# Eight pairs prepared on TensorE, staged early, with the next pair's PV blocks put off by one iteration

## The chip, the cores and the metric

The kernel runs on one core of a Trainium2 chip. The metric is the device time of the whole program in microseconds (us). The profile's span, from the first to the last instruction, is 1.8 us shorter than the time of the same execution. A program on one core has no die to compare with; a run is called slow when it is over 1.5% above the fastest run of the same kernel. Comparisons of times here use fast runs. A ratio is the mean time of one kernel's fast runs over the mean of the other's fast runs of the same rounds on the same chip, so it is not quite the ratio of the medians that are quoted.

## The reference

Attention over 8 batches and 8 heads, with q pooled in pairs of rows, then a feed-forward network (FFN) without an activation:

```python
q_pool = q.reshape(B, H, S // 2, 2, D).mean(axis=3)       # 8 x 8 x 576 x 64
scores = (1 / sqrt(D)) * q_pool @ k.T                     # 576 x 1152 per head
attn = softmax(scores)
x = (attn @ v), heads put side by side                    # 4608 x 512
a, b = x @ w1, x @ w2                                     # 4608 x 1024
out = ((a * b) @ w3) @ w_out                              # 4608 x 512
```

## The kernel before

Heads go in 32 pairs, four pairs to a batch. Each pair has k (kT) and pooled q (qT) transposed, then scores, exponentials (ScalarE), PV (the product with v) and a normalization. The main loop has 162 iterations. Each issues two chunks of scores and of exponentials, the PV blocks whose exponentials are ready, and as a filler some matmuls of the FFN, counted out by a pace in us. One `po` tile holds PV's sums, two `psc` tiles the scores, two `ff` banks everything else.

```python
def prep_dma(P):                      # pairs 6 to 31: transposed by DMA
    new_kq(P)
    kc = ab.tile([128, NJ, 2, D], FP16, tag="kc", bufs=2, name="kc")
    nc.vector.tensor_copy(out=kc..., in_=kst.pop(P))
    nc.sync.dma_start_transpose(out=kT[P], in_=kc...)
    pool_q(P)                         # VectorE adds neighbouring rows
    nc.sync.dma_start_transpose(out=qT[P], in_=qps[pp][o:o + 64]...)
    copy_v(P)

def prep_pe(P):                       # pairs 0 to 5: transposed on TensorE
    new_kq(P); pool_q(P)
    kc = ...; nc.vector.tensor_copy(out=kc..., in_=kst.pop(P))
    ...                               # 9 transposes of q, 9 of k into two ff banks
    nc.vector.tensor_copy(out=qT[P]..., in_=t2[:, 128:704])
    ...                               # kT blocks 0 to 7, block 8
    copy_v(P)

for it in range(NIT):
    ...                               # scores, expo, twice
    due = (due if filler else busy - T_SC) + (PACE0 if it < 20 else PACE1)
    lead = 0.5 if prepped < NPE else 2.0
    if prepped < NP and it * 2 * CH >= (prepped - lead) * PAIR + 2 * CH:
        if prepped < NPE:
            fill(0, settle=True)
        prep(prepped)
        ...                           # loads of a later pair
    for J, i in ready:
        attend(J, i)                  # PV
        if J % NJ == NJ - 1 and i == 4:
            normalize(J // NJ)
            fill(due)
    fill(due)
```

(Cuts are marked with `...`.) `qp` is the pooled q, `kc` the k put in order, `xn` the normalized sums of PV, `xT` the same transposed, which the FFN reads; `gT` is a * b, and T the product of w3 and w_out. `NPE` is the number of pairs that go through TensorE. After the loop come the last PV, what is left of the FFN and two FFN units that need the last batch (the tail).

The softmax here doesn't subtract the row's maximum and nothing guards it: scores larger than these inputs give would overflow.

## Time and profile before

| | before |
|---|---|
| time, 4 runs | 464.77 us median (460.99 to 467.72) |
| span of the profiled run | 462.8 us, mean granted TensorE clock 0.987 |
| TensorE busy | 422.5 us |
| ScalarE busy | 329.8 us |
| TensorE waits for the DMA that makes qT | 8.7 us, once |

How to read it: TensorE's busy time is 91% of the span. ScalarE has 29% to spare, so what counts is where TensorE waits. The prediction below shows the lines. A further line of the profile before, which the prediction did not use, is needed later. It is from the view of busy time by stretches: the stretch in us, its length, then busy time and count of instructions by engine, then the granted TensorE clock, the DMA share and GB/s.

```profile
61.70:65.10 3.40, 2.96 (x29) 2.27 (x29) 2.17 (x5) 0.46 (x1) 0.80 (x2) 0.50 1.18 208
...
95.80:102.60 6.80, 2.87 (x27) 1.65 (x27) 0.00 (x0) 1.94 (x2) 0.00 (x0) 0.50 1.26 144
```

Apart from its start and end, the program ran TensorE at half its clock (0.50) twice, both in the ramp: during the preparation near 62 us, and at the end of and after the wait for qT.

### The profile page before, as it was taken

The numbers are of one execution on the slowest core, as the hardware profiler recorded it, in microseconds if no ns is written. First come the engines' busy times: TensorE is split into PE (matmuls) and PEld (weight loads), VectorE is DVE, ScalarE is ACT, GpSimd is POOL, SyncE is SP. The second block draws the span as 40 slices with busy tenths as digits, with TensorE's granted clock in tenths as the row PEclk, the third lists the DMA queues.
The fourth block names the chain that finished last, engine by engine and source line by source line (L and its number), as shares of the span: only waits on it lengthen the run. The fifth ranks groups of instructions, "written<-read, shape, count | busy, mean of one in ns | idle before, by whom it ended". The sixth has DMA issues, their size and how long they took to land.

```text
span 462.8 us, 11974 instructions
## 1 busy us (share of the span) xinstructions
PE 422.5 (91%) x5132; PEld 222.4 (48%) x5132; DVE 195.6 (42%) x340; ACT 329.8 (71%) x350; POOL 69.6 (15%) x107
## 2 busy tenths in 40 slices
PE   2868888839999999999999999999999999999995
PEld 1544445425555555555555555555555555544442
DVE  2243355405544544355435543554355434444130
ACT  3868646728888888888888888888888888813332
POOL 7322112201111111111111111111100000000000
PEclk9999989979999999999999999999999999999999
DMA  8999996998999989999979999989973251022303
GB/s 135 209 192 208 208 205 84 147 137 115 122 123 201 154 138 117 165 182 137 145 141 171 133 127 177 172 111 142 183 138 52 53 120 38 15 58 47 77 15 91
DMA packets 98052, 59.99 MB, mean 130 GB/s; under 512 B 69840, under 2 KB 87248, under 8 KB 98000
## 3 DMA queue, kind: packets, MB, share of 16 engines
q0 software_dynamic: 25168, 33.56, 47.4%
q1 hardware_dynamic: 72832, 25.68, 35.8%
q8 instruction: 40, 0.66, 0.6%
q14 instruction: 12, 0.10, 0.1%
HBM read 67.11 MB, written 9.44 MB: 165 GB/s over the span
## 4 chain that ended last, share of the span: by engine, by line
PE 80%; DVE 9%; DMA 5%; ACT 3%; issue 2%; POOL 0%; ACTq 0%; POOLq 0%
PE po L204 22%; PE psc L185 20%; PE pp L299 12%; PE pa L276 12%; PE pb L289 11%; DVE xn L216 5%; DMA qT<-qp 4%; ACT er L191 2%; PE pT L263 2%; DVE rz L214 1%; DMA kst<-in_k_dram 1%; PE w3t L248 1%; DVE kT L162 1%; DVE qT L158 1%; DVE qp L119 0%
## 5 line engine op out<-in xcount | busy, mean ns | idle before, releaser
L191 ACT ACTIVATE er<-psc 128x1024 f16<-128x1024 f32 x324 | 313.4, 1021 | 83.6 <-PE psc L185 79.6
L204 PEld LDWEIGHTS <-er 128*128 128x128 f16 x2880 | 99.2, 98 | 55.3 <-issue 35.9
L185 PE MATMUL psc<-qT,kT 64*128 64x512 f16 (+7 forms) x1152 | 109.5, 291 | 15.0 <-DMA qT<-qp 8.7
L185 PEld LDWEIGHTS <-kT 64*128 64x128 f16 x1152 | 43.3, 95 | 88.3 <-issue 72.6
L289 PE MATMUL pb<-xT,w2sb 128*128 128x512 f16 x288 | 79.7, 379 | 0.7 <-DVE gT L294 0.7
L276 PE MATMUL pa<-xT,w1sb 128*128 128x512 f16 x288 | 80.0, 381 | 0.0
L294 DVE TENSOR_TENSOR gT<-pb,asb 128x512 f16<-128x512 f32 x72 | 49.6, 689 | 69.0 <-PE pb L289 68.6
L299 PE MATMUL pp<-T_73,gT 128*128 128x512 f16 x288 | 70.1, 379 | 0.0
L285 DVE COPY asb<-pa 128x512 f32<-128x512 f32 x56 | 38.6, 689 | 55.3 <-PE pa L276 55.2
L90 POOL DMA_DIRECT2D kst<-in_k_dram x32 | 22.9, 715 | 231.1 <-DVE kc L135 195.5
L308 DVE TENSOR_SCALAR osb<-pp 128x512 f32<-128x512 f32 x28 | 19.3, 691 | 57.0 <-PE pp L299 53.7
L289 PEld LDWEIGHTS <-w2sb 128*128 128x128 f16 x288 | 25.7, 97 | 24.1 <-issue 1.7
L299 PEld LDWEIGHTS <-gT 128*128 128x128 f16 x288 | 25.5, 97 | 24.5
L276 PEld LDWEIGHTS <-w1sb 128*128 128x128 f16 x288 | 25.8, 98 | 23.1 <-issue 0.3
L204 PE MATMUL po<-vt_78,er 128*128 128x65 f16 x720 | 30.6, 195 | 2.3 <-DVE xn L216 1.8
L204 PE MATMUL po<-vt_77,er 128*128 128x65 f16 x720 | 31.3, 197 | 1.0 <-DVE xn L216 0.6
L204 PE MATMUL po<-vt_79,er 128*128 128x65 f16 x720 | 30.1, 193 | 1.6 <-DVE xn L216 1.1
L204 PE MATMUL po<-vt_80,er 128*128 128x65 f16 x720 | 29.8, 194 | 1.2 <-DVE xn L216 0.9
L283 ACT COPY asb<-pa 128x512 f32<-128x512 f32 x16 | 9.4, 587 | 27.5 <-PE pa L276 27.5
L216 DVE TENSOR_TENSOR xn<-po,rz 128x640 f16<-128x640 f32 x32 | 26.4, 824 | 1.1
L97 POOL DMA_DIRECT2D vst<-in_v_dram x32 | 23.2, 724 | 15.6 <-DVE rz L214 5.3
L214 DVE RECIPROCAL rz<-po 128x10 f32<-128x10 f32 x32 | 7.1, 221 | 33.5 <-PE po L204 33.5
(68 smaller groups left out, 142.2 us busy)
## 6 DMA issues: line engine op xcount, KB each, us to landing
qst<-in_q_dram POOLq DMA_DIRECT2D x32, 288.0 KB, 6.3
kst<-in_k_dram POOLq DMA_DIRECT2D x32, 288.0 KB, 4.9
vst<-in_v_dram POOLq DMA_DIRECT2D x32, 288.0 KB, 8.8
out_dram<-osb SPq DMA_DIRECT2D x72, 128.0 KB, 3.5
w3h<-in_moe_w_dram POOLq DMA_DIRECT2D x2, 1024.0 KB, 19.9
wosb<-in_moe_w_out_dram POOLq DMA_DIRECT2D x1, 1024.0 KB, 19.6
xT<-xn SPq DMA_TRANSPOSE x64, 4.2
w1sb<-in_moe_w_dram POOLq DMA_DIRECT2D x1, 1024.0 KB, 20.8
```

The source lines that it names most:

```text
L90: nc.gpsimd.dma_start(out=kst[P].rearrange("p u j d -> p u (j d)"), in_=k[b, h0:h0 + 2].rearrange("u (p j) d -> p u (j d)", j=NJ))
L97: nc.gpsimd.dma_start(out=vst[P].rearrange("p u j d -> p u (j d)"), in_=v[b, h0:h0 + 2].rearrange("u (p j) d -> p u (j d)", j=NJ))
L185: nc.tensor.matmul(t[:, u, o:o + ln], kT[P][s, j, :], qv[s, f0:f0 + ln], start=True, stop=True)
L191: nc.scalar.activation(out=er[:, :, r:r + CH], in_=psc.pop(c), func=AF.Exp, bias=0.0, scale=SCALE)
L204: nc.tensor.matmul(po[P][:, u, VW * i:VW * i + D + 1], er[:, u, r:r + 128], vts[P % 4][:, u, j, 0:D + 1], start=(j == 0 and i == 0), stop= ...
L216: nc.vector.tensor_tensor(out=xn.rearrange("p i u d -> p u i d"), in0=acc[:, :, :, 0:D], in1=rz.to_broadcast([128, 2, 5, D]), op=ALU.mult)
L276: nc.tensor.matmul(pa, w1sb[:, mc, ft * 128:ft * 128 + 128], xT[:, mc, t0:t0 + 512], start=(mc == 0), stop=(mc == NC - 1))
L285: nc.vector.tensor_copy(out=asb, in_=pa)
L289: nc.tensor.matmul(pb, w2sb[:, mc, ft * 128:ft * 128 + 128], xT[:, mc, t0:t0 + 512], start=(mc == 0), stop=(mc == NC - 1))
L294: nc.vector.tensor_mul(out=gT[:, ft, :], in0=pb, in1=asb)
L299: nc.tensor.matmul(pp, gT[:, ft, 128 * i:128 * i + 128], T16[:, ft, :], start=(ft == 0), stop=(ft == NF - 1))
L308: nc.vector.tensor_scalar_mul(out=osb, in0=pp, scalar1=1.0 / (SCL * SCL))
```

## The change

The intent is to take three waits away. Two batches (eight pairs) are prepared on TensorE, so the first DMA transposes come later, after the early rush of loads. VectorE's part of a preparation is issued about an iteration before TensorE's. When a pair ends, the next pair's first PV blocks wait for the next iteration, so TensorE has the FFN and the next scores to do while VectorE normalizes. The filler gets a higher pace early on, and `T_AT`, the iterations at which the two halves of T enter it, starts one earlier.

```diff
-    NPE = 6
-    T_AT = (9, 14)
+    NPE = 8
+    T_AT = (8, 14)
-    PACE0, PACE1 = 1.95, 2.19
+    PACE0, PACE1 = 2.2, 2.19
+    def prep_stage(P):
+        pool_q(P)
+        kcs[P] = ab.tile([128, NJ, 2, D], FP16, tag="kc", bufs=2, name="kc")
+        nc.vector.tensor_copy(out=kcs[P]..., in_=kst.pop(P))
+        copy_v(P)
     def prep_pe(P):
-        ...                                  # pool_q, kc and copy_v were here
-        for j in range(NJ):
+        for j in (8, 0, 1, 2, 3, 4, 5, 6, 7):   # t2 is complete first
     ...
+        at = it * 2 * CH / PAIR
+        if staged < NPE and at >= staged - 0.8:
+            prep_stage(staged)
+            ...                              # loads
+        lead = 0.5 if prepped < NPE else min(1.6, 0.5 + 0.5 * (prepped - NPE + 1))
+        if prepped < NP and at >= prepped - lead:
+            ...                              # prep_pe, or prep_dma and one load
+        last = [n for n, (J, i) in enumerate(ready) if J % NJ == NJ - 1 and i == 4]
+        if last:
+            ready = ready[:last[0] + 1]
         for J, i in ready:
             attend(J, i)
-            if J % NJ == NJ - 1 and i == 4:
-                normalize(J // NJ)
-                fill(due)
+        if last:
+            normalize(ready[-1][0] // NJ)
```

More of the change, by code (lines that the diff above doesn't have):

```diff
@@ L140, in prep_dma @@
         copy_v(P)
+    kcs = {}
+    def prep_stage(P):
+        pool_q(P)
+        kcs[P] = ab.tile([128, NJ, 2, D], FP16, tag="kc", bufs=2, name="kc")
+        nc.vector.tensor_copy(out=kcs[P].rearrange("p j u d -> p u j d"), in_=kst.pop(P))
+        copy_v(P)
     def prep_pe(P):
@@ L145, in prep_pe @@
         new_kq(P)
-        pool_q(P)
-        kc = ab.tile([128, NJ, 2, D], FP16, tag="kc", bufs=2, name="kc")
-        nc.vector.tensor_copy(out=kc.rearrange("p j u d -> p u j d"), in_=kst.pop(P))
+        kc = kcs.pop(P)
+        t2 = psum.tile([128, 1024], FP16, tag="ff", bufs=2, name="t2")
         t1 = psum.tile([128, 1024], FP16, tag="ff", bufs=2, name="t1")
-        t2 = psum.tile([128, 1024], FP16, tag="ff", bufs=2, name="t2")
         for c in range(NJ):
@@ L163, in prep_pe @@
         nc.vector.tensor_copy(out=kT[P][:, 8], in_=t2[:, 0:128])
-        copy_v(P)
-    def prep(P):
-        (prep_pe if P < NPE else prep_dma)(P)
     psc = {}
@@ L334 @@
                lambda: load(5), lambda: load(6)]
-    loaded, prepped = 7, 1
-    prep(0)
+    loaded, staged, prepped = 7, 1, 1
+    prep_stage(0)
+    prep_pe(0)
     n_units = NT // 512
@@ L371 @@
         due = (due if filler else busy - T_SC) + (PACE0 if it < 20 else PACE1)
-        lead = 0.5 if prepped < NPE else 2.0
-        if prepped < NP and it * 2 * CH >= (prepped - lead) * PAIR + 2 * CH:
-            if prepped < NPE:
-                fill(0, settle=True)
-            prep(prepped)
-            prepped += 1
+        at = it * 2 * CH / PAIR
+        if staged < NPE and at >= staged - 0.8:
+            prep_stage(staged)
+            staged += 1
             if waiting:
@@ L381 @@
                     waiting.pop(0)()
-            elif loaded < NP:
+            else:
                 load(loaded)
                 loaded += 1
+        lead = 0.5 if prepped < NPE else min(1.6, 0.5 + 0.5 * (prepped - NPE + 1))
+        if prepped < NP and at >= prepped - lead:
+            if prepped < NPE:
+                fill(0, settle=True)
+                prep_pe(prepped)
+            else:
+                prep_dma(prepped)
+                load(loaded)
+                loaded += 1
+            prepped += 1
         ready = [b for b in blocks[nb:nb + 40]
                  if b[0] * SQ + min(128 * b[1] + 128, SQ) <= 2 * it * CH]
+        last = [n for n, (J, i) in enumerate(ready) if J % NJ == NJ - 1 and i == 4]
+        if last:
+            ready = ready[:last[0] + 1]
         busy += T_AV * len(ready)
```

## The prediction

> **What bounds the kernel now.** I read first the page's busy shares and its slices, then the chain that ended last, then TensorE's waits, and last the timeline around the waits. Of the page's parts 1, 2 and 4:
>
> ```profile
> PE 422.5 (91%) x5132; PEld 222.4 (48%) x5132; DVE 195.6 (42%) x340; ACT 329.8 (71%) x350; POOL 69.6 (15%) x107
> ...
> PE   2868888839999999999999999999999999999995
> ACT  3868646728888888888888888888888888813332
> ...
> PE 80%; DVE 9%; DMA 5%; ACT 3%; issue 2%; POOL 0%; ACTq 0%; POOLq 0%
> ```
>
> TensorE (PE) carries the chain and is full from the tenth slice (104 us) on. ScalarE's exponentials need 324 x about 1.0 us, and run at eight tenths up to slice 35. So the end is TensorE's work plus whatever time TensorE loses. The losses are in three places.
>
> (a) The first transposes made by DMA. TensorE's waits have one large line, and the chain in order of time shows what it hangs on:
>
> ```profile
> PE psc L185 <- DMA qT<-qp: 8.7, 1, 8.7
> ...
> 81.56 18.13 DMA qT<-qp
> 99.73 0.71 PE psc L185 x6
> ```
>
> Pair 6 (of 32 pairs of heads; the first six are transposed on TensorE) is the first to go by DMA. Its qT was issued at 81.56 and landed at 99.69, while loads of three pairs (kst, qst, vst, issued 76.7 to 86.2) were in flight. Everything stood still from 91.0 to 99.7.
>
> (b) The preparations on TensorE in the ramp. The timeline of the last of them (line, engine, output<-input, count, in brackets the idle time before and who ended it):
>
> ```profile
> 74.47 0.69 DVE L267 CAST T_73<-pT 128x512 f16<-128x512 f32 x1 [3.08 <-PE pT L263]
> 75.19 0.76 DVE L119 TENSOR_TENSOR qp<-qst 64x1152 f16<-64x1152 f16 x1
> ...
> 76.00 0.43 PE L152 MATMUL t_1142<-ident,qp 64*128 64x64 f16 x9 [1.57 <-DVE qp L119]
> ...
> 78.32 0.62 PE L248 MATMUL w3t<-ident,w3h 128*128 128x128 f16 x8 [0.61 <-DVE kT L162]
> ...
> 79.80 1.94 ACT L191 ACTIVATE er<-psc 128x1024 f16<-128x1024 f32 x2 [3.87 <-PE psc L185]
> ```
>
> VectorE starts pooling q only when the preparation is due, behind the eviction at 74.47, and TensorE waits 1.57 us for it and 0.61 for the copies afterwards; ScalarE misses 3.87.
>
> (c) The end of each pair. PV of the next pair follows in the same iteration and waits for the normalization, which frees the only po tile:
>
> ```profile
> 233.11 0.24 PE L204 MATMUL po<-vt_77,er 128*128 128x65 f16 x2
> ...
> 233.19 1.02 PE L299 MATMUL pp<-T_73,gT 128*128 128x512 f16 x4
> 233.39 0.22 DVE L214 RECIPROCAL rz<-po 128x10 f32<-128x10 f32 x1 [2.51 <-PE po L204]
> 233.64 0.82 DVE L216 TENSOR_TENSOR xn<-po,rz 128x640 f16<-128x640 f32 x1
> ...
> 234.52 0.66 PE L204 MATMUL po<-vt_78,er 128*128 128x65 f16 x16 [0.31 <-DVE xn L216]
> ```
>
> From the last PV to the next pair's first are 1.4 us, and only four FFN matmuls (0.86 us at their pace) fill them. The printed 0.31 is too small, as ends are modelled; measured by starts 0.47 is lost.
>
> **What the Trainium skill says.** "Perfetto Trace Analysis", Identifying the Most-Contended Engine: TensorE's busy share is no measure of its distance from the peak. The trace agrees: PE shows 91%, yet a matmul of 512 columns (mean 380 ns) starts 216 ns after the one before. So I count starts. "TensorE: Matmul & The Clock Gate", Back-to-back issue gap, gives N/2.4 + 2.5 ns as the isolated gap (216 at N=512), and 131 as sustained: here it is 216 (in the tail 32 take 6.91 us), so the latter isn't seen. The same page, PE-mode transpose, says that the result lands in PSUM and costs a VectorE copy; here one transpose's record is 190 to 220 ns but they start 29 (q) and 56 (k) ns apart, and the copies are 0.46 + 0.68 + 0.21 us. "DMA: Bandwidth & Descriptors", Issuing engines are not separate DMA queues: all queues share 16 engines and interleave. The trace agrees: transposes of k land in 3.3 us at the end, where no load runs, and in 13.1 beside three.
>
> **The change part by part.** The times of iterations are my count of the trace: iteration n starts with the first of its score matmuls. Iteration 0 starts at 9.33, 8 at 26.98, 31 at 103.16, 161 at 403.77; the last PV at 406.15, the end 462.8.
>
> Startup. VectorE now copies v of pair 0 before qT. That load lands at 8.77, so qT ends near 8.8 + 0.45 + 0.46 = 9.7 and kT's last block at 9.9, where ScalarE's kT copy (to 9.27) was last. Cost 0.6: start 9.9.
>
> Iterations 0 to 7 have no filler, so ScalarE sets the pace, 2.0 to 2.05. The before's took 17.65 with 1.2 lost at the first normalization and some 0.3 at the preparation; without them 16.5. Iteration 8 starts at 26.4.
>
> Iterations 8 to 30. From steady iterations of before: one with 5 FFN matmuls and 18 PV takes 2.27, each FFN matmul more or less 0.216, each PV 0.029. One with four takes 2.06, but then the next second score waits 0.2 for ScalarE. Replaying the two kernels' loops for what each iteration issues gives the counts: the changed kernel has five preparations here (iterations 8, 13, 18, 23, 28; before four), 64 w3 transposes and 94 FFN and T matmuls by the end of iteration 30 (before 78: iteration 8 starts T earlier, and pace 2.2 for 1.95 adds). Summed with 0.77 a preparation (9 x 29 + 9 x 56 ns) and 56 ns a w3 transpose: 56.7 us, against 54.3 for before. Waits come on top. Before: 76.2 - 54.3 = 21.9, of which about 10 in iteration 30 are (a), 10 the four preparations (1.7, 2.1, 3.4, 2.8) and 1.5 normalizations. After: q and k lie pooled and copied an iteration early, and qT's copy starts after 10 of the 18 transposes; what stays is the wait for the eviction of one ff bank before the t1 transposes (about 0.6) and for the copies after (about 0.55): 5 x 1.15, plus 1 for w3 transposes: 6.8. So 56.7 + 6.8 = 63.5, and iteration 31 starts at 89.9 rather than 103.16: 13 us gained, while 16 more FFN matmuls are done.
>
> Iterations 31 to 160. Before: 300.6 for 130, of which the 26 with a normalization average 2.54 and the others 2.255. After, the iteration that ends a pair stops PV there and has 5 to 7 FFN matmuls, and the scores of the next, before the next PV: 5 x 0.216 + 0.54 = 1.6 against the 1.4 of the normalization, so no wait. All go at 2.255: 26 x 0.285 = 7.4 gained. Added: the last preparation on TensorE, 0.77 + 1.15 = 1.9. And pair 8, first by DMA, starts in iteration 36 while its scores are the second of iteration 40, 4 x 2.27 + 0.27 = 9.4 us later. In before, beside one pair of loads, kT is issued 1 us after and lands 9.7 after its issue (107.83 to 117.53), qT 0.6 later: 11.3. I charge 2. Some banks wait behind the normalization: 1. Sum: 300.6 - 7.4 + 1.9 + 2 + 1 = 298.1. Iteration 161 starts at 388.
>
> Tail. 16 FFN matmuls fewer: 59.0 - 3.5 = 55.5 from there. 25 matmuls (5.4 us) remain between the last PV and the first that needs the last pair, whose xT landed 4.9 after the last PV: no wait.
>
> End 388.0 + 55.5 = 443.5, that is 19 us less in the profile. As the small waits are guesses from what others took, and a count of this kind misses some, I take 16.5: 466.24 - 16.5 = 449.7.
>
> **The rivals.** (1) Pair 8 takes over the wait of pair 6: its lead of 4.5 iterations is the shortest of all (later pairs have 7.6). If loads 12 and 13 slow the transposes as in (a), 13 to 18 us, the wait is 4 to 9 us, and the time 453 to 457. Against it: the loads are one pair per preparation now, not three within 10 us. (2) ScalarE or the loads bound the ramp: the loads of pairs 5 and 6 land only at 59.4 and 64.0 (the queue is full up to 70), and a staging that waits for one blocks VectorE. I have their stagings at 65 and 77, so they just fit; also the first FFN matmul, at 75, against xT of pair 3 at about 73. If both fail: 453. (3) What (c) frees comes back as waits for ScalarE, as with four-matmul iterations: then the 7.4 shrink to 3, time 454. Against: ScalarE needs 2.0 in 2.255. (4) PE really sets all and TensorE's added 36 transposes (1.5 us) are a loss: only if the waits in (a) and (b) stayed, which the order of instructions speaks against.
>
> **Range and chances.** One rival alone leaves 453 to 457, so the upper end is 457; if no new wait comes, 445. 2% faster is 456.9. Before's own runs spread from 460.99 to 467.72, which blurs this. Faster by over 2%: 0.88; within: 0.11; slower: 0.01.
>
> **What would show it.** Right: no wait of TensorE for qT over 3 us, and the one there is near iteration 40 (about 110 us); transposes of q never behind qp; no wait of po for xn; iteration 31 near 90 us; full PE from about slice 3 on; ACT's exponentials ending near 391 instead of 407. Wrong: a DMA wait of over 4 us, VectorE waiting for kst or vst landings, a mean iteration over 2.28 from 31 on.

## The result, and the profile after

The changed kernel takes 450.95 us (median of 4 runs, 449.94 to 451.36), against 464.77. The ratio is 0.9704, with a 95% interval of 0.9625 to 0.9783: faster. Every run was fast. The page of its profile (span 448.8 us), parts 1, 2 and 4; PEclk is the granted clock in tenths:

```profile
PE 419.4 (93%) x5168; PEld 223.1 (50%) x5168; DVE 198.2 (44%) x347; ACT 329.8 (73%) x350; POOL 70.0 (16%) x107
...
PE   2889898998699999999999999999999999989995
ACT  2977776777388888888888888888888888823332
PEclk9999999999699999999999999999999999999999
...
PE 83%; DMA 5%; ACT 4%; DVE 4%; issue 3%; SPq 1%; POOL 0%; ACTq 0%; DVEq 0%; POOLq 0%
```

VectorE's share of the chain fell from 9% to 4%. DMA still has 5%. The weak slices of the ramp have filled, but the eleventh (112 to 123 us) has a new dent, in PE, in ACT and in the clock. What that is, TensorE's waits and the chain in order of time tell (start, length, what):

```profile
PE psc L187 <- DMA qT<-qp: 5.3, 1, 5.3
```

```profile
103.02 12.49 DMA qT<-qp
...
115.65 0.61 PE psc L187 x2
```

It is the same wait as before, now for pair 8, at iteration 40. Its cost is more than the 5.3 us. The view by stretches shows TensorE idle, and then at half clock for two windows of 3.4 us:

```profile
110.50:114.50 4.00, 0.00 (x0) 0.00 (x0) 0.08 (x1) 1.02 (x1) 0.00 (x0) 1.00 1.57 106
114.50:121.40 6.90, 5.75 (x45) 2.78 (x46) 0.62 (x2) 2.71 (x3) 0.00 (x0) 0.51 1.27 136
```

Iterations 40 and 41 take 9.00 and 3.32 us, where two usual ones take 4.5. So 7.8 us go there. The Trainium skill ("TensorE: Matmul & The Clock Gate", What's actually happening) says that an idle window of about 3.4 us halves TensorE's clock and that a busy one restores it. The trace agrees for this wait: TensorE is idle from 111.1 to 114.5, then at half clock for 6.8 us, of which the last 3.4 are busy. It also shows that the window need not be idle throughout: the stretch of 3.4 us at half clock near 62 us in before follows 3.40 us in which TensorE was busy for 1.64.

The preparation that answers to the one in the prediction (timeline, pair 3) looks like this:

```profile
38.36 0.76 DVE L119 TENSOR_TENSOR qp<-qst 64x1152 f16<-64x1152 f16 x1
...
39.14 0.46 DVE L148 COPY kc<-kst 128x1152 f16<-128x1152 f16 x1
...
41.59 0.43 PE L158 MATMUL t_684<-ident,qp 64*128 64x64 f16 x9
41.69 0.69 DVE L269 CAST T_73<-pT 128x512 f16<-128x512 f32 x1 [1.72 <-PE pT L265]
...
42.44 0.61 PE L163 MATMUL t_685<-ident,kc 128*128 128x128 f16 x8 [0.25 <-DVE T_73 L269]
```

q and k lie ready 2 us before their transposes. The transposes of q wait for nothing; those of k wait 0.25 us for the eviction of a bank, where before TensorE lost 1.57 for qp. The end of a pair:

```profile
211.03 0.72 PE L206 MATMUL po<-vt_80,er 128*128 128x65 f16 x18
211.58 1.03 PE L301 MATMUL pp<-T_73,gT 128*128 128x512 f16 x4
211.78 0.22 DVE L216 RECIPROCAL rz<-po 128x10 f32<-128x10 f32 x1 [0.93 <-PE po L206]
212.04 0.82 DVE L218 TENSOR_TENSOR xn<-po,rz 128x640 f16<-128x640 f32 x1
212.54 0.82 PE L187 MATMUL psc<-qT,kT 64*128 64x128 f16 x8
...
213.29 0.66 PE L206 MATMUL po<-vt_77,er 128*128 128x65 f16 x16
```

The scores of the next iteration now stand between the last PV and the next pair's first, and no wait for xn is printed. In the whole trace one is left (0.2 us), where there were 11 (4.5 us).

Where the 14.0 us of the span went, by the starts of iterations (the first score matmul of each):

| stretch | before | after | difference |
|---|---|---|---|
| up to iteration 0 | 9.33 | 9.90 | +0.6 |
| iterations 0 to 7 | 17.65 | 16.10 | -1.6 |
| iterations 8 to 30 (after: 16 more filler matmuls) | 76.18 | 62.20 | -14.0 |
| iterations 31 to 160 | 300.61 | 304.86 | +4.3 |
| from iteration 161 (after: 16 fewer) | 59.03 | 55.74 | -3.3 |

### The profile page after: what moved, and what is told of

Same layout as the page of the kernel before. It is cut to its first block, busy times and chain, and to the rows that moved or that the text cites. A ratio compares the mean times of both kernels' runs of the same rounds, so it can differ in the third digit from the quotient of the medians.

```text
span 448.8 us, 12036 instructions
## 1 busy us (share of the span) xinstructions
PE 419.4 (93%) x5168; PEld 223.1 (50%) x5168; DVE 198.2 (44%) x347; ACT 329.8 (73%) x350; POOL 70.0 (16%) x107
## 4 chain that ended last, share of the span: by engine, by line
PE 83%; DMA 5%; ACT 4%; DVE 4%; issue 3%; SPq 1%; POOL 0%; ACTq 0%; DVEq 0%; POOLq 0%
PE po L206 20%; PE psc L187 20%; PE pb L291 13%; PE pa L278 13%; PE pp L301 12%; ACT er L193 4%; PE pT L265 3%; DMA qT<-qp 3%; DMA vst<-in_v_dram 1%; DVE xn L218 1%; DVE kT L168 1%; PE w3t L250 1%; DMA out_dram<-osb 1%; DVE T_73 L269 0%; DVE osb L310 0%
## 5 line engine op out<-in xcount | busy, mean ns | idle before, releaser
L206 PEld LDWEIGHTS <-er 128*128 128x128 f16 x2880 | 97.5, 98 | 35.5 <-issue 32.0
L187 PEld LDWEIGHTS <-kT 64*128 64x128 f16 x1152 | 44.4, 95 | 96.0 <-issue 84.5
L278 PE MATMUL pa<-xT,w1sb 128*128 128x512 f16 x288 | 79.1, 379 | 1.2 <-DVE asb L287 0.7
L301 PE MATMUL pp<-T_73,gT 128*128 128x512 f16 x288 | 71.4, 384 | 0.0
L206 PE MATMUL po<-vt_80,er 128*128 128x65 f16 x720 | 29.6, 196 | 0.3 <-DVE xn L218 0.2
L206 PE MATMUL po<-vt_77,er 128*128 128x65 f16 x720 | 29.7, 195 | 0.0
L206 PE MATMUL po<-vt_78,er 128*128 128x65 f16 x720 | 28.7, 193 | 0.0
L206 PE MATMUL po<-vt_79,er 128*128 128x65 f16 x720 | 28.7, 193 | 0.0
L218 DVE TENSOR_TENSOR xn<-po,rz 128x640 f16<-128x640 f32 x32 | 26.4, 824 | 1.3 <-DVE rz L216 0.2
```

The source lines that it names most:

```text
L187: nc.tensor.matmul(t[:, u, o:o + ln], kT[P][s, j, :], qv[s, f0:f0 + ln], start=True, stop=True)
L206: nc.tensor.matmul(po[P][:, u, VW * i:VW * i + D + 1], er[:, u, r:r + 128], vts[P % 4][:, u, j, 0:D + 1], start=(j == 0 and i == 0), stop= ...
L218: nc.vector.tensor_tensor(out=xn.rearrange("p i u d -> p u i d"), in0=acc[:, :, :, 0:D], in1=rz.to_broadcast([128, 2, 5, D]), op=ALU.mult)
L278: nc.tensor.matmul(pa, w1sb[:, mc, ft * 128:ft * 128 + 128], xT[:, mc, t0:t0 + 512], start=(mc == 0), stop=(mc == NC - 1))
L301: nc.tensor.matmul(pp, gT[:, ft, 128 * i:128 * i + 128], T16[:, ft, :], start=(ft == 0), stop=(ft == NF - 1))
```

## The experiments

The theory: early staging shortens the ramp, the deferral of PV shortens every pair's end, more pairs on TensorE merely move the DMA wait to a later pair, and the loads are what makes it long. The rivals stand in the expectations. Times of each kernel are medians; before, in the same three jobs (e1 to e4, e5 to e10, e11 and e12), had 464.41, 465.49 and 465.53. The changed kernel was not run again in them, so a run is compared with it by the ratio to before or by the traces. The intervals of e2, e4 and e6 overlap that of the changed kernel (0.9625 to 0.9783); there the traces decide, and not the times.

**e1: the deferral alone, on the kernel before.**

```diff
+        last = [n for n, (J, i) in enumerate(ready) if J % NJ == NJ - 1 and i == 4]
+        if last:
+            ready = ready[:last[0] + 1]
         ...
         for J, i in ready:
             attend(J, i)
-            if J % NJ == NJ - 1 and i == 4:
-                normalize(J // NJ)
-                fill(due)
+        if last:
+            normalize(ready[-1][0] // NJ)
```

> Before with one part of the change alone: PV of the next pair moved to the next iteration. My account: the 26 pair ends in iterations 31 to 160 lose 0.28 us each, so that stretch falls from 300.6 to about 293.5, and the whole by 7 to 9 us (five or six pair ends of the ramp included); the DMA wait of about 9 us for pair 6 stays. Rival (waits for ScalarE take it back): a gain of 3 us or less, the stretch at 297 or more.

457.49 us (455.25 to 460.26), ratio 0.9878 (0.9814 to 0.9943): 5.7 us faster, clear of noise, though less than the 2% that the verdict "faster" asks for; 7 to 9 us were expected. The DMA wait stayed (9.3 us). Iterations 47 to 160, which hold no DMA wait in before, after, e1 or e2, took 258.7 us, against 263.2 before. So 22 pair ends gained 4.5 us. The deferral works, at some 70% of the size that the prediction would give for that stretch (22 x 0.285 = 6.3), and ScalarE did not take it back.

**e2: the change without the deferral.** The edit is e1's, the other way round.

> The changed kernel without that part: PV goes on in the same iteration after the normalization. My account: iterations 41 to 160 take 7 us longer, the whole 457 to 459 against 451. Rival: within 3 us of the changed kernel. TensorE's waits for xn come back in the profile in either case.

459.82 us (453.15 to 462.5), ratio 0.9847 (0.9733 to 0.9961), from two runs alone: the other two were slow. The verdict is unclear. The total is blurred besides: in its profile (of a fast run) the wait for qT is 1.4 us at most, but iteration 45 waits 4.8 us for xT instead. Iterations 47 to 160 are clear of both: 263.5 us, against 259.4 in the changed kernel, so 4.2 us for 22 pair ends. Of this stretch, the mean iterations in us:

| kernel | with a normalization (22) | the next (22) | the others (70) |
|---|---|---|---|
| before | 2.52 | 2.23 | 2.27 |
| e2 | 2.57 | 2.22 | 2.26 |
| after | 2.35 | 2.24 | 2.26 |
| e1 | 2.26 | 2.29 | 2.27 |

**e3: a longer lead for the first pairs by DMA.**

```diff
-        lead = 0.5 if prepped < NPE else min(1.6, 0.5 + 0.5 * (prepped - NPE + 1))
+        lead = 0.5 if prepped < NPE else 1.6
```

> The changed kernel with the lead 1.6 for pairs 8 and 9 too: pair 8's DMA transposes start in iteration 34 instead of 36. If what is left of the DMA wait is a matter of lead: TensorE's wait for qT (5.3 us in the profile) is gone, and with it the stretch at half clock after it, 6 to 8 us in all: 443 to 445. Rival (the transposes move into other loads and land later by as much): the wait stays at 3 us or more, 447 to 451.

450.53 us (450.06 to 451.09): as the changed kernel. The chain in order of time shows why:

```profile
99.89 16.78 DMA qT<-qp
```

qT of pair 8 was issued 3 us earlier and landed no earlier. The rival holds: lead won in this way is of no use. Lead by itself was not tested, because load 12 is issued with the preparation and moved forward too (its k at 98.76 instead of 101.90).

**e4: load 12 held until pair 8's qT has landed.**

```diff
                 prep_dma(prepped)
+                if loaded == 12:
+                    nc.gpsimd.tensor_copy(out=scr, in_=qT[8][:, 0, 0:1])
                 load(loaded)
```

> The changed kernel with the loads of pairs 12 and up held back until pair 8's qT has landed (GpSimd reads one column of it first). If the loads slow the transposes: kT and qT of pair 8 land about 3 to 5 us after their issue (3.3 and 2.9 are the shortest, with no load), no wait at iteration 40, 443 to 445, unless the late loads make pair 12 or 13 wait. Rival (the transposes are slow among themselves, six of them within 9 us): qT still lands 10 us or more after issue and the wait stays.

447.36 us (445.66 to 448.55), ratio 0.9654 (0.9602 to 0.9706). kT of pair 8 landed 3.4 us after its issue and qT 4.5 (before this edit 5.1 and 12.5), and the wait at iteration 40 is gone. So the loads slow the transposes. But the held loads came in a burst, and pair 7's xT landed 11.4 us after issue: a wait of 2.6 us at iteration 45. Iterations 45 and 46 took 8.9 us instead of 4.5, so over half of the gain was moved on.

**e5: before with eight pairs on TensorE, nothing else.**

```diff
-    NPE = 6
+    NPE = 8
```

> Before with eight pairs prepared on TensorE instead of six, nothing else: pair 8 starts its DMA transposes in iteration 35, pair 9 in 37. If the DMA wait is only moved on: TensorE waits 4 to 9 us for qT at iteration 40 instead of 30, the two more preparations cost 2 to 3 us each in the old way, and the time stays within 4 us of before (460 to 467). Rival (the prediction's reading that the wait shrinks to some 2 us): 456 to 459.

Three of its four runs were slow (472.61 to 475.22); the fast one took 465.15, within the 460 to 467 expected, but no basis for a verdict on the time. The profile fell in a slow run, so only its structure is used. TensorE's waits there:

```profile
PE t L152 <- DVE qp L119: 12.7, 6, 6.2
PE psc L185 <- DMA qT<-qp: 9.5, 1, 9.5
```

The wait is at iteration 40 (13.5 us long) instead of 30. It was moved; how long it is in a fast run is not shown. The preparations wait for qp as ever.

**e6: the change with late staging.**

```diff
-        if staged < NPE and at >= staged - 0.8:
+        if staged < NPE and at >= staged - 0.5:
+            fill(0, settle=True)
```

> The changed kernel with the pooling and copying of q, k and v issued in the same iteration as the transposes, after the filler is settled, as before did. My account: TensorE waits for qp again by 1 to 1.6 us at six preparations or so (not the first, where ScalarE sets the pace), iteration 31 starts 6 to 9 us later than in the changed kernel (88.2), the time 456 to 459. Rival (the fillers and ScalarE take it up): under 3 us.

457.27 us (454.84 to 458.42), ratio 0.9814 (0.9757 to 0.9871). Iteration 31 started at 93.14 us, 4.9 later than in the changed kernel, and iteration 33 took 4.54 instead of 3.37. TensorE waits for qp again, here at pair 3:

```profile
43.35 0.43 PE L158 MATMUL t<-ident,qp 64*128 64x64 f16 x9 [1.57 <-DVE qp L119]
```

So early staging is worth 6 us (4.9 + 1.2). The waits for qp, without the first, sum to 6.5 us. The time is within what was expected; iteration 31 alone, with 4.9 instead of 6 to 9, is below it. (The loads that follow a staging are issued later in this edit as well; the waits printed are for VectorE.)

**e7: the change with the old pace.**

```diff
-    T_AT = (8, 14);  PACE0, PACE1 = 2.2, 2.19
+    T_AT = (9, 14);  PACE0, PACE1 = 1.95, 2.19
```

> The changed kernel with the old pace 1.95 up to iteration 20 and T starting at iteration 9. 16 FFN matmuls fewer are done by iteration 161 (695 against 711). If they were put into time that TensorE would have lost: 3 to 3.5 us longer (454). Rival (they only move time from the tail to the ramp): within 1 us.

454.14 us, but from 447.69 to 462.24, with two of four runs slow: the times cannot tell 3 us from 1. The profile, of a fast run, can. From iteration 0 to 31 it took 74.76 us, against 78.30 in the changed kernel: 3.5 less, for 16 filler matmuls fewer, and 16 x 0.216 = 3.5. The tail gets them back. The rival holds: the pace moved time from the tail to the ramp and gained nothing.

**e10: load 12 held until qT of pair 8, load 13 until xT of pair 7.**

```diff
                 prep_dma(prepped)
+                if loaded == 12:
+                    nc.gpsimd.tensor_copy(out=scr, in_=qT[8][:, 0, 0:1])
+                if loaded == 13:
+                    nc.gpsimd.tensor_copy(out=scr, in_=xT[:, 3, SQ + 511:SQ + 512])
                 load(loaded)
```

> The changed kernel with load 12 held until pair 8's qT and load 13 until pair 7's xT has landed. If contention with the loads is all: neither the qT wait at iteration 40 nor the xT wait at iteration 45 (2.6 us in the run that held load 12 alone), no stretch at half clock, 442 to 444. Rival (a burst of loads, later, makes something else wait): 446 or more.

443.51 us (442.6 to 444.65), ratio 0.9527 (0.9476 to 0.9577): faster than both kernels. GpSimd's wait, from the timeline, and the clock where the changed kernel stood still, from the view by stretches:

```profile
107.69 0.18 POOL L395 COPY scr<-qT 128x1 f16<-128x1 f16 x1 [12.32 <-DMA qT<-qp]
```

```profile
110.00:115.00 5.00, 4.97 (x59) 2.35 (x58) 2.22 (x5) 4.03 (x6) 0.22 (x1) 1.00 1.10 117
```

No iteration between 34 and 86 is over 2.6 us, and TensorE stays at full clock. The span is 441.2, that is 7.6 less than after, and 7.8 was the loss at iterations 40 and 41.

**e11: e10 with v of pair 0 copied later and the later pace 2.21.**

```diff
+        if P:
             copy_v(P)            # in prep_stage; copy_v(0) follows prep_pe(0)
-    PACE0, PACE1 = 2.2, 2.19
+    PACE0, PACE1 = 2.2, 2.21
```

> The kernel with the two held loads, v of pair 0 copied after its qT and kT, and the later pace 2.21 instead of 2.19, which puts 13 more FFN matmuls before iteration 161 (724). If such matmuls go into the time in which a short iteration makes the next score wait for ScalarE, up to 13 x 0.216 = 2.8 us shorter, and 0.4 at the start: 440 to 442. Rival (as the runs with the old pace suggest, a matmul costs its 0.216 us wherever it stands): 442.5 to 444.

447.82 us (fast runs 447.35 to 451.37), ratio 0.9633 (0.9585 to 0.968): worse than e10, and outside both expectations. TensorE's waits name what it is:

```profile
PE pb L293 <- DVE gT L298: 5.3, 7, 1.2
```

In e10 the like line has 1.2 us in 2 waits. In iteration 51, for one, the filler finishes one bank, fills a second and starts a third after the pair's last PV; the first one's eviction stands on VectorE behind the normalization, and TensorE waits 0.69 us. The pace also changes how the fillers fall (iterations 105, 125 and 145 have eight each). Iterations 20 to 46 took 70.6 us instead of 66.0, and 47 to 160 took 263.5 instead of 259.6. The 13 more matmuls are 2.8 us of these 8.5 and the tail gives them back; the rest is lost. The start at 9.51 is not told apart from the others: kernels with the order of before started between 9.3 and 10.2.

**e12: before with loads 9 and 10 held.**

```diff
+                if loaded in (9, 10):
+                    nc.gpsimd.tensor_copy(out=scr, in_=qT[loaded - 3][:, 0, 0:1])
                 load(loaded)
```

> Before with nothing changed but loads 9 and 10 held until qT of pairs 6 and 7 has landed. If the wait of iteration 30 is the loads' doing: qT of pair 6 lands within 6 us of issue, TensorE's wait for it and the half-clock stretch go, 10 us in iteration 30: 453 to 456, with six pairs on TensorE as before. Rival (moving two more pairs to TensorE is what removes it): the wait stays over 4 us, 460 or more.

464.82 us (20 runs), ratio 1.0029 (1.0001 to 1.0057): the same. qT of pair 6 landed 3.7 us after its issue and the wait at iteration 30 went, as the theory has it; but the delayed loads then met pair 9's transposes:

```profile
111.97 22.75 DMA qT<-qp
```

Iteration 45 took 11.2 us. The cause was right and the expected time wrong: holding loads without a place where they can be made up only moves the wait.

## Why the prediction was right or wrong

The time, 449.7, and the range, 444 to 457, held (450.95), and so did the expected direction. The gain over before's median of that day was 13.8 us, against 16.5. Of its own signs of being wrong, two came true all the same: a DMA wait of over 4 us (5.3), and a mean iteration over 2.28 from 31 on (2.345; without iterations 40 and 41 it is 2.285). The last exponentials ended at 395.5, not near 391. Point by point:

- **Startup.** 9.9 was expected and 9.90 found; but starts of kernels with unchanged order vary as much, so the reason given is not shown.
- **Iterations 0 to 7.** 26.4 expected for iteration 8, 26.00 found.
- **Iterations 8 to 30.** 89.9 expected for iteration 31, 88.20 found. The waits of the five preparations were smaller than the "5 x 1.15": by the same count they lost 1.0, 0.6, 1.0, 0.6 and 0.5. That VectorE's late start is the cause was shown by e6. Something the prediction missed helped: in before, the preparation near 62 us also ran at half clock, and in the changed kernel the clock stays full up to the wait at iteration 40. Whether a preparation meets such a stretch is not settled by the change, though: e12, with the preparations of before, has three such stretches in the ramp (at 26.1, 60.2 and 77.3 us), and e3, with those of the changed kernel, has one (at 25.1).
- **The pace.** The prediction counted 16 matmuls more in the ramp and 16 fewer in the tail, a sum of nothing, and e7 shows just that.
- **"All go at 2.255: 26 x 0.285 = 7.4 gained".** The mechanism was right, the size not. e1 and e2 give 4.5 and 4.2 us for 22 pair ends instead of 6.3. Iterations with a normalization started from 2.52 and not 2.54, and fell to 2.35, not to 2.255. Two of the 22 (87 and 117) take 2.85 and 3.26, where a bank's eviction stands behind the normalization on VectorE; the other 20 average 2.28. That is a wait which the prediction had as "some banks", 1 us. Rival (3), that what is freed comes back as waits for ScalarE, is not seen: the iterations without a pair's end are as long as before.
- **"I charge 2" for pair 8.** This term failed most. It cost 7.8 us: a wait of 5.3, and TensorE at half clock for 6.8 us around and after it. This is rival (1), which was put at 4 to 9 us. The reason given against it, that the loads are "one pair per preparation now, not three within 10 us", does not hold. Pairs 8 and 9 are prepared two iterations apart, GpSimd's loads start as soon as a buffer is free, and so loads 12 and 13 were issued from 101.9 to 107.0, beside four transposes. e4 and e10 show that the loads did it; e3 shows that more lead does not help while load 12 moves along.
- **The tail.** 55.5 expected, 55.74 found.

The sum of the steps was a span of 443.5; the trace has 448.8. The difference of 5.3 is +5.8 for pair 8, +2.4 for the deferral (26 x 4.2/22 = 5.0 gained instead of 7.4), -1.7 up to iteration 31, and -1.2 for the last preparation on TensorE, the bank waits and the tail. The allowance of 2.5 us for waits that such a count misses was right in sign, and too small. The start helped too: 16.5 was taken from 466.24, a median, while the run that was counted took 464.58, which would have given 448.1. So the nearness of 449.7 is in part luck: errors had opposite signs, and the base was on the high side.

What stays open: what eight pairs instead of six are worth alone (e5 has one fast run), and what the new order of the transposes and the earlier loads add, which no run took out singly. Further, why the size of the wait for qT varies so much between like kernels (2.8 us in e7's profile, 5.3 in the changed kernel's). It depends on how the loads and transposes meet, and no run fixed that apart from those that kept them apart.

## What to carry to other kernels

When a transfer that the critical engine waits for is late, look first at what else is in flight beside it, and only then at its lead: here two iterations more of lead, with a load moving along, gave nothing, and holding two loads back gave 7.6 us. Work that an idle engine does for the critical one should be issued before it is due, and not behind that engine's evictions. A long wait of TensorE costs more than its length, because the clock halves and takes a window to return; and a held transfer needs a place later where it can be made up, or the wait only moves.

## What the Trainium skill lacked or had wrong

- "TensorE: Matmul & The Clock Gate", Back-to-back issue gap, gives 131 ns as the sustained spacing at 512 columns. No stretch here shows it: 32 such matmuls in a row take 6.91 us, 216 ns each, which is the page's isolated figure.
- The same page, PE-mode transpose, gives about 275 ns for a transpose in a kernel. In a row they start 56 ns (128x128) and 29 ns (64x64) apart here; this section has no spacing, which is what a plan needs. (N/2.4 + 2.5, the gap of plain matmuls that the prediction quotes, gives the same two numbers.)
- The same page, What's actually happening, has the clock halved after an idle window. Here windows in which TensorE worked half of the time did it too: busy for 1.64 of 3.40 us in before (58.3 to 61.7, in part with transposes), and for 1.67 of 3.40 in e2 (128.3 to 131.7, without any).
- "DMA: Bandwidth & Descriptors" says that queues share the 16 engines, but has no figure for DMA transposes within SBUF beside loads. Here one of k or q (128 x 1152 or 64 x 1152) lands 3 to 4.5 us after issue when no load runs, 5 to 11 beside the loads of one pair as in most of before, and up to 15.2 (the changed kernel), 18.1 (before) and 22.8 (e12) where loads of two or more pairs and other transposes are in flight.
